# One written order for all five engines through the whole attention stage, with the engine of each copy named in it

## The chip, the cores and the metric

One core of one Trainium2 chip. The metric is the device time of one execution in microseconds (us), the median of the runs shown; lower is better. The engines are TensorE (PE; its weight loads are PEld), VectorE (DVE), ScalarE (ACT), GpSimd (POOL) and SyncE (SP), each of which works through its own instructions in order. DMAs are issued from the queues of SP, ACT and POOL.

## The reference

Three layers follow each other on 2304 = 4 x 576 rows, all in float32. This is `reference()`, cut to what is computed:

```python
# attention: 4 batches, 8 heads, 512 local and 32 global rows, head size 64, window 32
s_g   = scale * q_g @ concat(k_g, k_l).T            # global rows see everything
out_g = softmax(s_g) @ concat(v_g, v_l)
s_ll  = where(|i - j| <= 32, scale * q_l @ k_l.T, -1e9)
out_l = softmax(concat(scale * q_l @ k_g.T, s_ll)) @ concat(v_g, v_l)
x = concat(out_g, out_l) as [2304, 512]
# feed-forward 1, 1536 wide
xn = x / sqrt(mean(x*x) + 1e-6) * rms_g
x  = (silu(xn @ w_gate) * (xn @ w_val)) @ w_out
# feed-forward 2, 2048 wide
h  = x @ w_in
x  = ((a0 + a1*h + a2*h^2 + a3*h^3) / (1 + |b0||h| + |b1|h^2 + 1e-6)) @ w_out
```

The weights arrive as float64 and are turned on the chip into two float32r halves (the "conversion").

## The kernel before

The attention works in 32 stages (`Attention.place`): a stage is one pair of heads and 256 local rows. A stage has four steps on PE: `scores` (S, into a PSUM tile psS), `trans` (T, psT), `pv` (O, psO) and `out` (X, psX). Between them lie masks and sums on DVE, exponentials and copies on ACT. Once per batch `make_g` (psKG) turns the global keys and queries, eight times `g_scores`, `g_trans`, `g_pv` and `g_out` (psG, psGT, psOg, psGX) treat the global rows. Values lie in four buffers `vw`: `load_v` brings a stage's values to partitions 32 to 63, `spread_v` copies them to two other groups of 32 partitions (`vw<-vw`).

Beside it runs the first feed-forward layer (`FFN1`). Its work is cut into units: 12 matmuls of a gate and a value half (`up`, psg and psv), or 12 matmuls of a product with w_out (`down`, psA). 12 units make one of 8 blocks of rows for one of 3 groups of 512 columns. 58 units run inside the attention, so that PE has something dense to do while a stage waits. Before a block's first unit come its norm (`norm_stages`: psN, a small chain of DVE and ACT operations on the tile `sm`, psR, four scalings of x) and its split in two halves (`chunk`, xt).

The order is set in two ways. For the first 14 stages, 18 units, the conversion of the first 12 weights and three norms, a text `SCRIPT` (L857) is read token by token: `S4` is the first step of stage 4 on PE, `M4` its masks on DVE, `E4` its exponentials, `>q5` a load on SP's queue, `U` a unit, `n0` the next step of a norm. All five engines take their instructions in the order of the text. From stage 14 on, the loop at L1038 calls `flow` (L553), which puts loads, steps, units and norm steps one behind the other; PE and SP keep that order, while ACT, DVE and POOL are ordered by a list scheduler when the program is built. Which engine does a copy is fixed in the code: `spread_v` for stages 4 and up is two DMAs on SP's queue, psT and psX are emptied by ACT, psGT and psGX by DVE, the key blocks of the global rows are copied by POOL, and in the conversion `CONV_ON` (L879) names the engine for three of the operations.

```python
        self.advance(t - 1, 2)          # flow: T of the stage before
        between()                       # a unit
        self.advance(t, 1)              # S of this stage
        self.advance(t - 2, 4)          # X
        self.advance(t - 1, 3)          # O
        self.ready(t + 1)               # keys and queries of the next
        between()
        middle()                        # a step of a norm
```

After the attention the rest of the units, the conversion of the other weights and the second feed-forward layer are ordered by the list scheduler.

Of the kernel before, what the change touches and what calls it, by code (L numbers as in the profile page):

```python
# [10 lines left out]
F32 = mybir.dt.float32  # L11
# [9 lines left out]
S = SL + SG  # L21
# [25 lines left out]
class Weights:  # L47
# [30 lines left out]
    def stages(self, job, lo_eng, r8_act, sum_eng=None):  # L78
# [6 lines left out]
        if self.wide:  # L85
# [4 lines left out]
            if r8_act:  # L90
# [6 lines left out]
            nc.vector.tensor_scalar(out=vf, in0=vf, scalar1=TINY, scalar2=None, op0=ALU.max)  # L97
            nc.vector.tensor_scalar(
                out=v, in0=v, scalar1=3, scalar2=0x3FFFFFFF, op0=ALU.logical_shift_left, op1=ALU.bitwise_and
            )  # L100
            nc.vector.scalar_tensor_tensor(
# [3 lines left out]
            (sum_eng or nc.vector).tensor_tensor(out=v, in0=v, in1=lo, op=ALU.add)  # L105
        else:
            yield
            yield 1
            yield 1
# [5 lines left out]
        lo_eng.tensor_tensor(out=out[:, 1], in0=vf, in1=out[:, 0].bitcast(F32), op=ALU.subtract)  # L115
# [29 lines left out]

def pool_round(nc):
    return lambda out, in_: nc.gpsimd.tensor_scalar(  # L147
        out=out, in0=in_, scalar1=1.0, scalar2=1.0, op0=ALU.mult, op1=ALU.mult
    )


class Attention:
# [9 lines left out]
    def __init__(self, tc, pool, x, stage, q_l, k_l, v_l, q_g, k_g, v_g, ident):  # L162
        self.tc, self.nc, self.pool, self.x = tc, tc.nc, pool, x
# [159 lines left out]
    def make_k(self, r):  # L323
# [3 lines left out]
        if r < 4:  # L327
# [3 lines left out]
            nc.vector.tensor_copy(out, ps.rearrange("p (m i k) -> p m i k", i=2, k=32))  # L331
        else:
# [3 lines left out]
        nc.gpsimd.tensor_scalar(  # L336
            out=_ap(kt, [[32 * (KBLK - 8), 2], [32, 8], [1, 32]]), in0=_ap(kg, [[0, 2], [0, 8], [1, 32]]),
            scalar1=1.0, scalar2=1.0, op0=ALU.mult, op1=ALU.mult,
        )

    def make_q(self, s):
        nc = self.nc
        self.qts[s] = qt = self.pool.tile([128, 256], F32, tag="qt", name=f"qt{s}", bufs=2)
        if s < 8:
# [3 lines left out]
            nc.scalar.activation(out=qt, in_=ps[:, 0:256], func=AF.Copy)  # L348
# [55 lines left out]
    def trans(self, s):  # L404
# [5 lines left out]
        nc.scalar.activation(out=o, in_=ps, func=AF.Copy)  # L410

    def pv(self, s):
# [15 lines left out]
        nc.vector.reciprocal(out=dn, in_=dn)  # L428
        self.on[s] = on = self.work.tile([128, 4, D], F32, tag="on", name=f"on{s}", bufs=2)
        nc.vector.tensor_tensor(out=on, in0=ps[:, :, 0:D], in1=_ap(dn, [[1, 4], [0, D]]), op=ALU.mult)  # L430

    def out(self, s):
# [8 lines left out]
        nc.scalar.activation(out=xo, in_=ps[:, 0:256], func=AF.Copy)  # L441
# [25 lines left out]
    def g_trans(self, qd, part):  # L467
# [10 lines left out]
        nc.vector.tensor_copy(o[:, g0:g1], ps[:, 0 : 128 * (g1 - g0)].rearrange("k (n q) -> k n q", q=128))  # L478

    def g_pv(self, qd):  # L480
        nc, o, ps = self.nc, self.gq.pop(qd), self.bank(2, f"psOg{qd}")
        for n in range(5):
# [11 lines left out]
        nc.vector.reciprocal(out=gs[:, 0:1], in_=gs[:, 0:1])  # L494
        og = self.pool.tile([128, 2, D], F32, tag="og", name=f"og{qd}", bufs=1)
        self.gq[qd] = og
        nc.vector.tensor_scalar(
            out=og, in0=_ap(ps, [[0, 2], [1, D]]), scalar1=gs[:, 0:1], scalar2=None, op0=ALU.mult
        )

    def g_out(self, qd):
# [4 lines left out]
        for hf in range(2):  # L506
            rows = slice(64 * hf, 64 * hf + 64)
            src = ps[rows, 0:128].rearrange("d (p h i) -> d p h i", p=2, h=2)[:, :, hf, :]
            self.nc.vector.tensor_copy(self.x[b][hq][rows, :, 0:SG], src)

    def all(self, gen):
        for _ in gen:
            pass

    def advance(self, s, to):

        if not 0 <= s < self.NS:
            return
        while self.stage.get(s, 0) < to:
            now = self.stage[s] = self.stage.get(s, 0) + 1  # L520
            self.all((self.scores, self.trans, self.pv, self.out)[now - 1](s))
            if now == 3 and s + 4 < self.NS:
                self.load_v(s + 4)

    def ready(self, t):

        b, i = divmod(t, 8)
        if t >= self.NS:
            return
        if i < 4 and b:  # L530
            self.all(self.make_k(4 * b + i))
            if i < 2:
                self.load_k(4 * b + i + 2)
        self.all(self.make_q(t))

    def loads(self, t):

        b, i = divmod(t, 8)
        if t >= self.NS:
            return  # L540
        if t + 1 < self.NS:
            self.spread_v(t + 1)
        if b + 1 < B:
            if i == 4:
                self.load_g(b + 1)
            if i in (5, 6):
                self.load_k(4 * b + i - 1)
            if i >= 4:
                self.load_q(8 * b + i + 4)
        if t > 7 and i in (3, 4, 5):  # L550
            self.load_vn(4 * b + i - 3)

    def flow(self, t, between, middle):  # L553

        NS = self.NS
        b, i = divmod(t, 8)
        live = t < NS
        qd = 2 * b
        self.loads(t)
        self.advance(t - 1, 2)  # L560
        between()
        if live and i in (6, 7):
            self.all(self.g_pv(qd + i - 6))
            if i == 6:
                self.load_vn(2 * qd + 3)
        if live and i in (5, 6):
            self.all(self.g_trans(qd + i - 5, 0))
        self.advance(t, 1)
        if live and i in (5, 6):
            self.all(self.g_trans(qd + i - 5, 1))  # L570
        self.advance(t - 2, 4)
        self.advance(t - 1, 3)
        if live and i == 6 and b + 1 < B:
            self.all(self.make_g(b + 1))
        self.ready(t + 1)
        between()
        middle()
        if live and i in (4, 5):
            self.all(self.g_scores(qd + i - 4))
        if i == 0:  # L580
            self.all(self.g_out(qd - 1))
        if live and i == 7:
            self.all(self.g_out(qd))
        between()


class FFN1:
# [6 lines left out]
    def __init__(self, tc, pool, x, y, gam, wts, ident):  # L594
        self.tc, self.lo = tc, tc.nc.gpsimd
# [7 lines left out]
        self.norms, self.acts, self.split_of, self.pending, self.copies, self.defer = {}, {}, {0: {}, 1: {}}, {}, {}, True  # L603
# [21 lines left out]
    def norm_stages(self, blk):  # L625
# [7 lines left out]
        for c, q in ((1, r), (2, u), (3, r)):  # L633
            nc.scalar.activation(out=q, in_=self.xs(blk, c), func=AF.Square)
            yield
            self.lo.tensor_tensor(out=m, in0=m, in1=q, op=ALU.add)
# [40 lines left out]
    def chunk(self, grp, blk, c, xt):  # L677
# [6 lines left out]
        self.lo.tensor_tensor(out=t[:, 1], in0=v, in1=t[:, 0].bitcast(F32), op=ALU.subtract)  # L684
# [14 lines left out]
    def act(self, k, blk, pss, use_silu):  # L699
# [16 lines left out]
        self.lo.tensor_tensor(out=al, in0=a, in1=ah.bitcast(F32), op=ALU.subtract)  # L716

    def down(self, grp, blk, m):
# [12 lines left out]
        if grp == 0:  # L731
            nc.scalar.activation(out=y, in_=ps, func=AF.Copy)
# [123 lines left out]

SCRIPT = """  # L857
>k0 i1 i0 }q0 >g0 }q1 >k1 ]v0 tab i2 K0 >k2 i3 k0 Q0 q0 >q2 H0 h0 Q1 >k3 j0 z0 q1
S0 >w1 >v1 K1 M0 E0 k1 z1 s0 T0 S1 C0 GS0 M1 E1 >q3 Q2 GM0 K2 q2 O0 >w0 k2 z2
K3 GE0 >v2 N0 T1 S2 k3 z3 C1 a1 M2 X0 GS1 E2 s1 T2 Y0 >v3 GM1 l1 GT0 n0 C2 GC0  # L860
Q3 b1 GT1 q3 O1 GE1 S3 >v5 N1 a0 d1 l0 >w2 M3 X1 s2 E3 >w3 GC1 >c b0 T3 Y1 f1
>q4 C3 s3 O2 n0 d0 >n0 f0 N2 >v4 e0 n0 X2 O3 Y2 e1 n0 >q5 N3 Q4 n0 q4 >v6 a2
X3 S4 l2 a3 b2 >n1 Y3 l3 Q5 >s4 n0 q5 M4 n0 S5 E4 >q6 b3 d2 n0 >s6 T4 f2 >s5
n0 M5 GO0 d3 n0 C4 >w5 n0 E5 e2 O4 >q7 GN0 n0 f3 GT2 >q8 N4 GX0 e3 n0 GC2 GY0 X4
>n2 a5 l5 n0 GT3 Y4 n0 >w6 Q7 GC3 b5 >g1 q7 Q6 T5 q6 >w4 S7 C5 >v7 n0 d5 n0 x0
S6 x1 M7 >v8 x2 y0 O5 E7 M6 y1 H1 N5 T7 y2 x3 >v9 f5 U y3 h1 C7 Q8 e5 a4
j1 E6 >w7 U Q12 >s8 l4 b4 >k4 T6 a6 U l6 b6 C6 d4 u0 >s7 O6 f4 u0 U >w8 d6
>g2 N6 u0 e4 f6 K4 >w9 X5 u1 X6 >q9 Y5 O7 u1 e6 Y6 a7 U N7 l7 u0 a8 b7 >n3
# [278 lines left out]
```

## Time and profile before

| | us |
|---|---|
| median of 3 runs | 1016.77 (1015.79 to 1017.24) |
| the profiled execution: its own time | 1017.83 |
| the profiled execution: its span | 1016.0 |
| attention stage with its 58 units, up to | about 270 |
| TensorE clock granted, mean of the span | 0.97 |

The profiled execution lies 1.06 us above the median, and 1.83 us of its time lie outside the span. Shares of busy time are read by stretch, since the attention (0 to 270 us) and the feed-forward layers (270 to 1016 us) have little in common: in the second part PE is busy nearly all the time.

### The profile page before, as it was taken

The page shows a single profiled execution, that of the slowest core. Times are in us where ns is not written, and L with a number is a line of the kernel's source. Part 1 is how long each engine was busy: PE and PEld are TensorE (multiplying, and loading weights), DVE is VectorE, ACT ScalarE, POOL GpSimd, SP SyncE. Part 2 cuts the span into 40 slices and gives each one's busy share as a digit, 9 for nine tenths or more (in the row PEclk, how much of TensorE's full clock was granted, in tenths as well). Part 3 has the DMA queues.
Part 4 walks back from the last instruction along what each step waited for, and adds up shares of the span by engine and source line. Part 5 has one row for each costly group of instructions (what it writes and reads, how often), then busy time and mean ns, then how long its engine had stood idle before and what let it go on. Part 6 is the DMA issues. An engine that isn't in the chain of part 4 may idle for free.

```text
span 1016.0 us, 21488 instructions
## 1 busy us (share of the span) xinstructions
PE 957.9 (94%) x8224; PEld 877.4 (86%) x8224; DVE 778.3 (77%) x1856; ACT 578.9 (57%) x1319; POOL 279.5 (28%) x351
## 2 busy tenths in 40 slices
PE   6778998789999999999999999999999999999997
PEld 4576877677899999899999998888989899898995
DVE  6878555555698997738964535998998989989897
ACT  6566354345676765436632424666666666666674
POOL 6666132121200000000000012453543435434433
PEclk9587999789999999999999999999999999999999
DMA  8887665443535216404310135000000000000000
GB/s 176 209 174 163 131 127 119 103 96 80 181 132 166 85 63 209 166 1 167 125 43 1 43 96 195 1 1 32 1 1 32 1 18 15 1 32 1 1 32 21
DMA packets 132614, 82.24 MB, mean 81 GB/s; under 512 B 95424, under 2 KB 120032, under 8 KB 132512
## 3 DMA queue, kind: packets, MB, share of 16 engines
q1 hardware_dynamic: 129536, 74.02, 26.6%
q0 software_dynamic: 1888, 6.59, 2.0%
q8 instruction: 65, 1.06, 0.4%
q10 hardware_dynamic: 1088, 0.26, 0.1%
q14 instruction: 37, 0.30, 0.1%
HBM read 62.64 MB, written 10.75 MB: 72 GB/s over the span
## 4 chain that ended last, share of the span: by engine, by line
PE 64%; DVE 17%; DMA 7%; SPq 4%; ACT 4%; issue 2%; POOL 1%; ACTq 0%; DVEq 0%; POOLq 0%
PE psA L725 4%; PE psg L693 4%; PE psA L727 4%; PE psA L726 4%; PE psv L693 4%; PE psg L697 4%; PE psg L694 4%; PE psv L694 4%; PE psv L697 4%; SPq L215 4%; PE psH L804 4%; PE psH L805 4%; PE psH L806 4%; PE psB L839 4%; PE psB L840 3%; PE psB L841 3%
## 5 line engine op out<-in xcount | busy, mean ns | idle before, releaser
L804 PE MATMUL psH<-yt,w_h 128*128 128x384 f32 (+1 forms) x384 | 126.0, 329 | 1.2 <-ACT yt L786 0.7
L805 PE MATMUL psH<-yt,w_h 128*128 128x384 f32 (+1 forms) x384 | 125.4, 327 | 0.0
L806 PE MATMUL psH<-yt,w_h 128*128 128x384 f32 (+1 forms) x384 | 123.5, 328 | 0.8 <-DVE yt L787 0.8
L693 PE MATMUL psg<-xt,w_g 128*128 128x288 f32 (+1 forms) x384 | 116.3, 304 | 0.0
L725 PE MATMUL psA<-ah,w_o 128*128 128x288 f32 (+1 forms) x384 | 110.9, 293 | 5.4 <-ACT ah L714 2.8
L147 POOL TENSOR_SCALAR gh<-p 128x384 fp32r<-128x384 f32 (+1 forms) x96 | 57.7, 601 | 211.8 <-DVE p L828 178.4
L693 PE MATMUL psv<-xt,w_v 128*128 128x288 f32 (+1 forms) x384 | 112.2, 293 | 0.3 <-DVE gm L460 0.3
L839 PE MATMUL psB<-w_p,gh 128*128 128x512 f32 x272 | 107.8, 396 | 4.9 <-POOL gh L147 4.8
L694 PE MATMUL psg<-xt,w_g 128*128 128x288 f32 (+1 forms) x384 | 111.9, 292 | 0.0
L694 PE MATMUL psv<-xt,w_v 128*128 128x288 f32 (+1 forms) x384 | 111.9, 292 | 0.0
L726 PE MATMUL psA<-ah,w_o 128*128 128x288 f32 (+1 forms) x384 | 109.1, 288 | 0.0
L727 PE MATMUL psA<-al,w_o 128*128 128x288 f32 (+1 forms) x384 | 109.0, 288 | 0.0
L830 POOL TENSOR_TENSOR gl<-p,gh 128x384 fp32r<-128x384 f32 (+1 forms) x96 | 106.2, 1106 | 8.4 <-PE psB L841 0.5
L840 PE MATMUL psB<-w_p,gh 128*128 128x512 f32 x272 | 107.2, 394 | 0.0
L697 PE MATMUL psg<-xt,w_g 128*128 128x288 f32 (+1 forms) x384 | 106.0, 292 | 0.0
L697 PE MATMUL psv<-xt,w_v 128*128 128x288 f32 (+1 forms) x384 | 105.8, 293 | 0.0
L824 ACT ACTIVATE r<-q,cq 128x384 f32<-128x384 f32 (+1 forms) x96 | 57.4, 598 | 63.8 <-DVE q L814 63.0
L93 POOL TENSOR_SCALAR raw_h<-raw_h 128x512 int32<-128x512 uint32 x1 | 0.6, 647 | 328.4 <-DMA raw_h<-in_moe_w_in_dram 328.4
L814 DVE SCALAR_TENSOR_TENSOR q<-q,bv,t 128x384 f32<-128x384 f32 (+1 forms) x96 | 71.4, 744 | 22.5 <-ACT q L812 22.5
L841 PE MATMUL psB<-w_p,gl 128*128 128x512 f32 x272 | 82.0, 394 | 0.0
L725 PEld LDWEIGHTS psA<-ah,w_o 128*128 128x128 f32 x384 | 71.9, 188 | 7.8 <-ACT ah L714 3.5
L813 ACT ACTIVATE p<-psH,av 128x384 f32<-128x384 f32 (+1 forms) x96 | 62.7, 653 | 26.3 <-POOL gl L830 26.0
(173 smaller groups left out, 2638.5 us busy)
## 6 DMA issues: line engine op xcount, KB each, us to landing
raw_h<-in_moe_w_in_dram SPq DMA_DIRECT2D x16, 512.0 KB, 3.9
raw_p<-in_moe_w_out_dram SPq DMA_DIRECT2D x16, 512.0 KB, 3.9
vw<-vw SPq DMA_DIRECT2D x56, 130.0 KB, 2.4
raw_v<-in_moe_w_val_dram SPq DMA_DIRECT2D x12, 512.0 KB, 5.1
raw_g<-in_moe_w_gate_dram SPq DMA_DIRECT2D x12, 512.0 KB, 6.2
raw_o<-in_moe_w_out_dram SPq DMA_DIRECT2D x12, 512.0 KB, 3.9
vw<-in_v_l_dram SPq DMA_DIRECT2D x60, 80.0 KB, 2.7
out_dram<-o SPq DMA_DIRECT2D x17, 256.0 KB, 2.0
```

Source lines behind the costliest of these rows:

```text
L693: nc.tensor.matmul(ps[j], part(j, 0, c), xt[c][:, 0], start=(c == 0), stop=False)
L694: nc.tensor.matmul(ps[j], part(j, 1, c), xt[c][:, 0], start=False, stop=False)
L697: nc.tensor.matmul(ps[j], part(j, 0, c), xt[c][:, 1], start=False, stop=(c == 3))
L725: nc.tensor.matmul(ps, wh, ah, start=(i == 0), stop=False)
L726: nc.tensor.matmul(ps, wl, ah, start=False, stop=False)
L727: nc.tensor.matmul(ps, wh, al, start=False, stop=(i == 3))
L804: nc.tensor.matmul(ph[:, :n], wh, yt[:, c, 0, :n], start=(c == 0), stop=False)
L805: nc.tensor.matmul(ph[:, :n], wl, yt[:, c, 0, :n], start=False, stop=False)
L806: nc.tensor.matmul(ph[:, :n], wh, yt[:, c, 1, :n], start=False, stop=(c == 3))
L839: nc.tensor.matmul(acc[m], gh[:, sl], wh, start=(k == 0), stop=False)
L840: nc.tensor.matmul(acc[m], gh[:, sl], wl, start=False, stop=False)
L841: nc.tensor.matmul(acc[m], gl[:, sl], wh, start=False, stop=(k == NC2 - 1))
```

## The change

The text `SCRIPT` now covers all 32 stages, all 8 norms and all 58 units, and the five engines follow it to the end of the attention. `flow`, `ready`, `loads`, `advance` and the loop around them are gone. A token may end in `/A`, `/V` or `/P`, which names ACT, DVE or POOL for the operation (`self.eng`); `]` in front of a load names POOL's queue. Helper `put` writes the copy for the engine named. Each step of a conversion is now its own token. In the norm the first estimate r0 and its first refinement lie in PSUM (behind the sums in psN) and no longer in the SBUF tile `sm`.

```diff
+def put(nc, eng, out, in_):
+    if eng == "A":
+        nc.scalar.activation(out=out, in_=in_, func=AF.Copy)
+    elif eng == "V":
+        nc.vector.tensor_copy(out, in_)
+    else:
+        nc.gpsimd.tensor_scalar(out=out, in0=in_, scalar1=1.0, scalar2=1.0, op0=ALU.mult, op1=ALU.mult)
...
-            (sum_eng or nc.vector).tensor_tensor(out=v, in0=v, in1=lo, op=ALU.add)
+            (nc.gpsimd if self.eng == "P" else nc.vector).tensor_tensor(out=v, in0=v, in1=lo, op=ALU.add)
...
     def spread_v(self, s):
-            if s < 4:
-                self.nc.gpsimd.tensor_scalar(out=out, in0=in_, scalar1=1.0, scalar2=1.0, op0=ALU.mult, op1=ALU.mult)
+            if self.eng:
+                put(self.nc, self.eng, out, in_)
             else:
                 self.dma(out=out, in_=in_)
...
-        nc.scalar.activation(out=o, in_=ps, func=AF.Copy)
+        put(nc, self.eng or "A", o, ps)
...
-        nc.vector.tensor_tensor(out=on, in0=ps[:, :, 0:D], in1=_ap(dn, [[1, 4], [0, D]]), op=ALU.mult)
+        if self.eng == "A":
+            for i in range(4):
+                nc.scalar.activation(out=on[:, i], in_=ps[:, i, 0:D], func=AF.Copy, scale=dn[:, i : i + 1])
+        else:
+            nc.vector.tensor_tensor(out=on, in0=ps[:, :, 0:D], in1=_ap(dn, [[1, 4], [0, D]]), op=ALU.mult)
...
-        nc.scalar.activation(out=r, in_=m.bitcast(I32), func=AF.Exp, scale=-self.LN2H / 2**23, bias=self.eps)
+        r0 = ps[:, 4 : 4 + n]
+        nc.scalar.activation(out=r0, in_=m.bitcast(I32), func=AF.Exp, scale=-self.LN2H / 2**23, bias=self.eps)
...
-S6 x1 M7 >v8 x2 y0 O5 E7 M6 y1 H1 N5 T7 y2 x3 >v9 f5 U y3 h1 C7 Q8 e5 a4
+q7/V X5 t2 S7 Y5/A y3/P U M7 >n2 y2/P E7 d2/V >v8 H1 b5 f2 U h1 o5 e2/V T7 t5 u0 U a4 j1 >q6 C7/A d5/V l4/A >k4
...
-    manual.enter_context(tc.manual_schedule(engines={mybir.EngineType.PE, mybir.EngineType.SP}))
...
+        tc.manual_schedule(engines={getattr(mybir.EngineType, e) for e in ("PE", "SP", "Activation", "DVE", "Pool")})
...
-    for t in range(FLOW, LAST + 1):
...
-            att.flow(t, between, norm_step)
...
+    assert done[0] == IN_ATTN
```

PE, the norm of block 4, before: the sums (psN) and the spread of the result over the partitions (psR) stand next to each other, between a unit (psg, psv) and the turning of stage 26's probabilities (psT). The same holds for blocks 2, 5 and 7.

```order
L697 MATMUL psg_3_3478<-xt_2_3_2780,w_g_1058 128x288
L697 MATMUL psv_3_3479<-xt_2_3_2780,w_v_1178 128x288
L641 MATMUL psN_3582<-ones,st_4_3459 128x1 x3
L657 MATMUL psR_3595<-ident,sm_3586 128x128 x2
L657 MATMUL psR_3595<-ident,sm_3586 128x32
L407 MATMUL psT_3607<-ident,p_3516 128x128 x4
```

And after, around the same block's psN, where a transposition of the global rows and their product (psOg) follow:

```order
L495 MATMUL psGT_1_4175<-ident,pg 128x128 x2
L455 MATMUL psX_4182<-ident,on_4170 128x128 x2
L590 MATMUL psN_4187<-ones,st_4_4031 128x1 x3
L526 MATMUL psGX_4194<-ident,og_4151 128x128
L503 MATMUL psOg_4196<-vn_105,ptg_4146 32x64 x2
```

Its psR comes 37 rows later, behind psOg (20 matmuls), a unit of block 5, another psGX and a second unit:

```order
L648 MATMUL psv_2_4222<-xt_5_2_3536,w_v_975 128x256
L648 MATMUL psg_2_4221<-xt_5_3_3577,w_g_1053 128x256
L648 MATMUL psv_2_4222<-xt_5_3_3577,w_v_975 128x256
L608 MATMUL psR_4271<-ident,sm_4217 128x128 x2
L608 MATMUL psR_4271<-ident,sm_4217 128x32
```

For blocks 2, 5 and 7 it comes 60, 63 and 120 rows later; nothing stands next to its own psN any more.

SP's queue, before, around the loads of the queries of batch 3 (x_0_76) and of the keys (kin): spreads (`vw<-vw`) stand in front of both.

```order
L215 DMA vw_100<-vw_100 32x2x520 x2
L215 DMA gin<-in_k_g_dram 32x8x64
L215 DMA gin<-in_q_g_dram 32x8x64
L215 DMA x_0_76<-in_q_l_dram 32x16x32 x4
L215 DMA vn_103<-in_v_l_dram 128x2x256
L215 DMA vn_103<-in_v_g_dram 32x2x64
L215 DMA vw_102<-in_v_l_dram 32x10x64 x2
L215 DMA vw_101<-vw_101 32x2x520 x2
L215 DMA kin_88<-in_k_l_dram 32x16x32 x4
```

After, the same loads on SP's queue:

```order
L232 DMA vw_101<-in_v_g_dram 32x8x64 x2
L232 DMA kin_88<-in_k_l_dram 32x16x32 x4
L232 DMA x_1_75<-in_q_l_dram 32x16x32 x4
L232 DMA vw_100<-in_v_l_dram 32x10x64 x2
L232 DMA x_1_77<-in_q_l_dram 32x16x32 x4
L232 DMA x_0_76<-in_q_l_dram 32x16x32 x4
```

and on POOL, which did no DMAs in this stretch before, loads and spreads between the subtractions of the units:

```order
L667 TENSOR_TENSOR al_3_2214<-a_3_2212,ah_3_2213 128x288
L232 DMA vw_102<-in_v_l_dram 32x10x64 x2
L232 DMA vw_102<-in_v_g_dram 32x8x64 x2
L232 DMA vw_101<-vw_101 32x2x520 x2
L667 TENSOR_TENSOR al_0_2305<-a_0_2303,ah_0_2304 128x256
L159 TENSOR_SCALAR vw_102<-vw_102 32x2x520 x2
L232 DMA kin_88<-in_k_l_dram 32x16x32 x4
L585 TENSOR_TENSOR st_2_2291<-st_2_2291,st_2_2293 128x288
```

Counted over the program, SP issues 114 DMAs fewer: 88 went to POOL's queue (20 of kin, 40 of values and global values to vw, 14 of vn, 14 spreads) and 26 spreads became copies. Of the 64 spread copies and DMAs 30 are DMAs now (56 before), 20 copies on POOL (8) and 14 on ACT (0).

## Rows read from the trace of the kernel before

**Rows 1.** The page: span, TensorE's granted clock in 40 slices of 25.4 us.

```profile
span 1016.0 us, 21488 instructions
PEclk9587999789999999999999999999999999999999
```

**Rows 2.** Busy time by stretch: length, PE, PEld, DVE, ACT, POOL, clock, DMA share, GB/s.

```profile
0.00:122.00 122.00, 96.16 (x1410) 76.10 (x1410) 90.43 (x311) 69.75 (x182) 67.01 (x91) 0.83 0.78 173
122.00:270.00 148.00, 130.05 (x2089) 111.78 (x2086) 78.66 (x354) 70.35 (x204) 37.39 (x52) 0.93 0.46 101
270.00:1016.00 746.00, 731.72 (x4733) 689.53 (x4731) 609.20 (x1191) 438.82 (x934) 175.13 (x209) 1.00 0.18 62
```

**Rows 3.** Waits of PE, 122 to 270 us: waiter, awaited: sum us, times, longest.

```profile
PE psR L657 <- DVE sm L652: 8.6, 4, 2.8
PE psKG L356 <- ACT x L441: 2.1, 1, 2.1
PE psX L436 <- DVE x L509: 1.3, 1, 1.3
```

**Rows 4.** Time line of PE at block 4's norm: start, length, instruction, idle before.

```profile
218.17 0.72 PE L641 MATMUL psN<-ones,st 128*128 128x1 f32 x6
221.70 1.46 PE L657 MATMUL psR<-ident,sm 128*128 128x128 f32 x6 [2.81 <-DVE sm L652]
```

**Rows 5.** The three stretches at half clock after 122 us (columns of rows 2).

```profile
155.65:159.06 3.41, 3.41 (x19) 3.41 (x19) 1.79 (x4) 0.60 (x1) 0.00 (x0) 0.50 0.00 0
186.37:196.61 10.24, 8.39 (x65) 8.06 (x67) 4.07 (x15) 1.30 (x3) 1.66 (x3) 0.50 0.41 85
220.50:227.33 6.83, 5.63 (x54) 5.31 (x54) 2.78 (x7) 0.60 (x1) 0.64 (x1) 0.50 0.10 31
```

**Rows 6.** Time line of PE where the clock falls, at 186.4 us.

```profile
185.98 0.29 PE L694 MATMUL psg<-xt,w_g 128*128 128x288 f32 x1
186.11 0.29 PE L693 MATMUL psv<-xt,w_v 128*128 128x288 f32 x1
...
186.60 0.45 PE L694 MATMUL psg<-xt,w_g 128*128 128x288 f32 x1
186.84 0.45 PE L693 MATMUL psv<-xt,w_v 128*128 128x288 f32 x1
```

**Rows 7.** Chain of waits that ended last, 180 to 186 us: start, length, what.

```profile
180.79 0.49 SPq L215
...
181.32 2.25 DMA kin<-in_k_l_dram
...
185.35 0.46 PE psKG L356 x4
```

**Rows 8.** DMA issues up to 270 us: queue, count, KB each, median us to landing.

```profile
vw<-in_v_l_dram SPq DMA_DIRECT2D x60, 80.0 KB, 2.7
vw<-in_v_l_dram POOLq DMA_DIRECT2D x2, 80.0 KB, 3.7
```

**Rows 9.** Spreads, 0 to 270 us: ns least/median/most of one, first and last start.

```profile
L215 SPq DMA_DIRECT2D vw<-vw x56: 591/596/1640, 32.1 to 238.8; - x56
L304 POOL TENSOR_SCALAR vw<-vw x8: 1048/1054/1398, 8.4 to 26.4; 32x1040 f32<-32x1040 f32 x8
```

**Rows 10.** Groups of POOL, 0 to 270 us: busy us, mean ns, idle before.

```profile
L716 POOL TENSOR_TENSOR al<-a,ah 128x256 fp32r<-128x256 f32 x12 | 9.1, 762 | 15.6 <-PE psA L727 10.9 <-ACT ah L714 4.6
L105 POOL TENSOR_TENSOR cv<-cv,raw_o 128x512 int32<-128x512 int32 x4 | 5.5, 1370 | 2.1 <-POOL al L716 0.7 <-DVE cv L101 0.7 <-issue 0.7
L215 POOL DMA_DIRECT2D vw<-in_v_l_dram x2 | 1.5, 738 | 0.0
```

**Rows 11.** Groups of DVE: up to 122 us (first row), over the whole span (others).

```profile
L105 DVE CUSTOM_DVE_ANT_0 cv<-raw_g,cv 128x1024 uint16<-128x1024 uint16 x1 | 1.3, 1319 | 0.1
...
L684 DVE TENSOR_TENSOR xt<-x,xt 128x256 fp32r<-128x256 f32 x36 | 14.6, 418 | 3.2 <-ACT xt L682 3.2
L105 DVE CUSTOM_DVE_ANT_0 cv<-raw_o,cv 128x1024 uint16<-128x1024 uint16 x8 | 5.5, 684 | 0.0
```

More of the change, by code (lines that the diff above doesn't have):

```diff
@@ L494, in g_pv @@
         nc.vector.reciprocal(out=gs[:, 0:1], in_=gs[:, 0:1])
+        yield
         og = self.pool.tile([128, 2, D], F32, tag="og", name=f"og{qd}", bufs=1)
         self.gq[qd] = og
-        nc.vector.tensor_scalar(
-            out=og, in0=_ap(ps, [[0, 2], [1, D]]), scalar1=gs[:, 0:1], scalar2=None, op0=ALU.mult
-        )
+        two = _ap(ps, [[0, 2], [1, D]])
+        if self.eng == "A":
+            nc.scalar.activation(out=og, in_=two, func=AF.Copy, scale=gs[:, 0:1])
+        else:
+            nc.vector.tensor_scalar(out=og, in0=two, scalar1=gs[:, 0:1], scalar2=None, op0=ALU.mult)
     def g_out(self, qd):
@@ L508, in g_out @@
             src = ps[rows, 0:128].rearrange("d (p h i) -> d p h i", p=2, h=2)[:, :, hf, :]
[L509 to L584, printed above, removed]
+            put(self.nc, self.eng or "V", self.x[b][hq][rows, :, 0:SG], src)
@@ L602, in __init__, with pick @@
         self.ident = ident
-        self.norms, self.acts, self.split_of, self.pending, self.copies, self.defer = {}, {}, {0: {}, 1: {}}, {}, {}, True
+        self.norms, self.acts, self.split_of, self.pending, self.copies, self.defer = {}, {}, {i: {} for i in range(TASKS)}, {}, {}, True
+    def pick(self):
+        return {"V": self.nc.vector, "P": self.nc.gpsimd}.get(self.eng, self.lo)
     def set_psum(self, pp, gv, acc):
@@ L1005 @@
             att.spread_v(n)
-        elif name in ("a", "l", "b", "d", "f", "e"):
+        elif name in "abdefolt":
             if name == "a":
-                pick = [{"A": None, "P": nc.gpsimd, "V": nc.vector}[e] for e in CONV_ON[n]]
-                conv[n] = wts.stages(jobs[n], pick[2], not pick[0], pick[1])
+                conv[n] = wts.stages(jobs[n], nc.gpsimd, True)
             next(conv[n], None)
@@ L1019 @@
             next(phases["x", n], None)
-        elif name in ("U", "D"):
+        elif name == "U":
             unit()
         elif name == "W":
-            next(ffn.copies[1, n], None)
+            next(ffn.copies[divmod(n, 4)], None)
         elif name == "u":
@@ L1030 @@
             next(phases[then[name], n], None)
-    for s in range(FLOW):
-        att.stage[s] = sum((n, s) in phases for n in "STOX")
-    begin.close()
     ffn.defer = False
@@ L1036 @@
         assert next(rest, 0) == 0
-    base = done[0]
-    for t in range(FLOW, LAST + 1):
-        for _ in range(2):
-            wts.step(nc.gpsimd)
-        if t < HALF:
-            target[0] = base + (EARLY - base) * (t + 1 - FLOW) / (HALF - FLOW)
-        else:
-            target[0] = EARLY + (IN_ATTN - EARLY) * (t + 1 - HALF) / (LAST + 1 - HALF)
-        with tc.high_priority(offset=50):
-            att.flow(t, between, norm_step)
-        while done[0] < target[0] - 1:
-            unit()
-        if t % 4 == 1:
-            norms.append(ffn.norm(ORD[(t - 5) // 4]))
-        with tc.high_priority(offset=200):
-            norm_step()
-    while done[0] < IN_ATTN:
-        unit()
+    att.eng = ffn.eng = wts.eng = None
+    assert done[0] == IN_ATTN
     manual.close()
```

127 lines of the change are left out of this document (75 added, 52 removed).

## The prediction

> **What bounds the kernel now.** I read the shares by stretch first [rows 2]. From 270 us on PE is busy for 731.72 of 746 us at full clock; the change touches nothing there and I expect the same time. What can be won lies before: in the first 122 us, which already follow a written order, PE is idle for 122 - 96.2 = 25.8 us and the granted clock is 0.83; from 122 to 270 us, where the list scheduler orders ACT, DVE and POOL, it is idle for 148 - 130.1 = 17.9 us and the clock is 0.93. In that second stretch no other engine is near its limit: DVE is busy for 78.7 of 148 us, ACT for 70.4, POOL for 37.4, and the DMAs have a share of 0.46. So it is not work that holds PE up there, but the order in which short steps wait for each other.
>
> The waits of PE say which [rows 3]: 8.6 us in four waits of psR for the small chain of the norm (`sm`, L652), 2.1 us in one wait of psKG for ACT and 1.3 us in one of psX for DVE; together 12.0 of the 17.9 us. One of them in the time line [rows 4]: psN starts at 218.17 and lasts 0.72 us, psR starts at 221.70, after 2.81 us of idleness. Nothing is late in it; the chain through DVE and ACT takes 2.8 us, and PE's own order has nothing else to do in between. It costs a second time through the clock [rows 1, 5]: after 122 us PE is at the lower level, 1.2 GHz, in three stretches of 20.48 us together, with 17.4 us of busy PE in them, and each begins at such a place. The one from 155.65 follows a wait of psR, the one from 186.37 follows the wait of psKG and holds another psR, the one from 220.50 lies in the wait of rows 4.
>
> **The change, part by part.** The norms first. In the new order of PE the four psR that stood next to their psN stand 37 to 120 rows behind it, with two units or more, or the steps of several stages, between. A unit is 12 matmuls of 256 or 288 columns, and at full clock one starts 0.13 us after the other [rows 6], so two units are 24 x 0.13 = 3.1 us, more than the longest of the four waits. I take 8.0 of the 8.6 us as gone; the bounds are 4 us (DVE and ACT reach the chain late, because they too have other things in their lists) and 8.6. Late next is what needs the scaled x, the split of a block whose units come later, and those have units of the block before them as cover. That the norm's r0 goes to PSUM I cost at nothing: the chain is covered, and without that cover it would cost at most what it costs today.
>
> The clock. Two matmuls are 0.13 us apart at full clock and 0.24 us apart at the lower level [rows 6]. If the three stretches vanish, 17.4 us of busy PE become 17.4 x 0.13 / 0.24 = 9.4 us: 8.0 us at most, and 0 at least, if other gaps pull the clock down in their place. The new order has its own thin places: between units 46 and 47 nine steps of stages follow each other without a unit. One dip of the size of the last (5.6 us of busy PE, 2.6 us of loss) I leave standing: 8.0 - 2.6 = 5.4 us.
>
> The loads. The wait of psKG hangs on a chain that starts in SP's queue [rows 7]: SP issues one DMA after the other at half a microsecond each, the keys' load starts only at 181.32 and takes 2.25 us, the DVE waits for it with all that is behind it, and psKG starts at 185.35. SP loses 114 issues; the 40 spreads among them at 0.596 us [rows 9] and the others at 0.49 us [rows 7] are 23.8 + 36.3 = 60 us of queue time, and the loads of queries and keys no longer stand behind spreads that wait for a stage's pv. I take 3 us of the 2.1 + 1.3 us [rows 3]; bounds 0 and 3.4.
>
> What it adds. POOL issues 88 DMAs at 0.74 us [rows 10], 65 us, and makes 12 spreads more at 1.05 us [rows 9], 12.6 us; it loses 30 subtractions and sums of norms at about 0.76 us and 9 sums of the conversion at 1.37 us [rows 10], 35 us, and 8 key copies, at a spread's 1.05 us at most 8.4 us. Its 104 us of work before 270 us [rows 2] become about 140: room is left. DVE takes on the 30 subtractions at 0.42 us, 12.5 us, and 9 sums at 0.68 to 1.32 us [rows 11], 6 to 12 us, with copies of 4000 columns net that I price by the same 0.42 us for 256 columns, 6.5 us: its 169 us [rows 2] become about 195 to 200. Over 253 us that is 78%, and in the first stretch it goes from 90.4 to about 97 to 102 of 122 us. That is the cost that I trust least; for the first stretch as a whole I take 0, with -10 us (its idle time and its lower clock are both larger than after 122 us, and the loads come earlier) and +10 us (the DVE's work lies wholly on the path) as bounds. ACT's 14 spreads appear in no row on that engine. The nearest is POOL's, 1.05 us, which I take: 15 us, on an engine that is busy for 140 of 270 us [rows 2]; half of it and twice it change nothing.
>
> Sum: 8.0 + 5.4 + 3 + 0 = 16.4 us off the profiled execution's 1017.83 us. It lies 1.06 us above the median, so for the median 1016.8 - 16.4 = 1000.4, rounded to **1000 us**. About 0.2%, 2 us, is what a measurement of this kernel can tell from no change.
>
> **The rivals.** (a) The first stretch gains as well. Its 25.8 us of idle PE and its clock of 0.83 (0.17 x 122 = 21 us of clock not granted) are larger than all that I count after 122 us, and now every engine's place in it is chosen anew. A third of them, about 15 us, on top gives 985. Against it: the DMAs (0.78 of the time) and DVE (90.4 of 122 us) are near their limit there [rows 2], and DVE gets more.
>
> (b) DVE becomes the bound. If the 7 to 12 us that it gains in the first stretch come out on PE, and some waits for copies that ACT made before come on top, of 16.4 us some 4 are left: 1013. For it speaks that one list for DVE holds work of five kinds, each of which can stand in front of the other; against it, that DVE has 148 - 78.7 us free after 122 us.
>
> (c) POOL's queue is late, and the kernel is slower. A stage's values and keys are now often loaded from POOL's queue, where they stand behind subtractions that wait for units, and a load that waits for a buffer holds up the subtractions behind it, on which the next units hang. The two such loads in the trace took 3.7 us to land, against 2.7 from SP [rows 8], and issuing costs 0.74 us of POOL's own time. If each of the 18 stages after the fourteenth waits 1.5 us for this, that is 27 us: 16.4 - 27, thus 1027 us. It decides from 16.4 / 1.5 = 11 late stages on. Against it: SP's spread of a stage took part in the waits, too, and most of POOL's loads stand some stages ahead of their use. The Trainium skill ("SBUF — State Buffer", section "SBUF: two separate sides") has a rule that speaks for it: descriptors of a DMA issued from GpSimd are written by that engine's own cores, which are locked out while VectorE runs an operation that takes both ports, so that the transfer starts late; it advises SP's or ACT's queue. By that rule the time would be that of (c); by the trace, where the two loads land 1.0 us later, loads that are issued some stages ahead hide it and the sum stays. Two loads are few to tell the two apart.
>
> (d) That the change does not do what it says can be left out: the orders above show the moved instructions.
>
> **How the numbers follow.** The forecast has 0.55: its own range, from the bounds of its three terms with a third of the bounds of the first stretch (4 + 2 + 0 to 8.6 + 8 + 3.4 + 3), goes from 994 to 1011. (a) has 0.20, (b) 0.13, (c) 0.12. Faster by over 0.2% are the forecast, (a) and half of (b): 0.82. Within 0.2% lies 0.06 of (b); slower are (c) and no more: 0.12. For 8 in 10 the range takes in (a) down to 982 and (b) up to 1015 and leaves out (c) and the far end of (a).
>
> **What would show it.** Right: PE waits of psR after 122 us under 1 us in all; no wait of psKG behind a load of keys; clock at 0.97 or more from 122 us to the end of unit 58, and that end at about 253 us instead of 270; from there on 746 us as before; DVE near 195 us by then. Wrong: psT, psO or psS waiting for DVE or POOL by more than 8 us in all; DMA landings from POOL's queue in the chain of waits; a clock in the second stretch that is no better than 0.93; or an end of the first stretch that moves by more than 10 us in either direction.

## The result and the profile after

| | before | after |
|---|---|---|
| median of the runs beside each other, us | 1016.28 (4 runs) | 1000.54 (4 runs, 998.86 to 1005.71) |
| ratio, with its 95% interval | | 0.985 [0.981, 0.989] |
| the same comparison on a second chip | 1019.04 (11 runs) | 1001.22 (6 runs), 0.983 [0.979, 0.986] |
| profiled execution: span, us | 1016.0 | 997.4 |

The kernel is faster by 1.5%, and the forecast of 1000 us and its range hold. The page of the changed kernel, where [rows 1] stood before:

```profile
span 997.4 us, 21577 instructions
PEclk9788999999899999999999999999999999999999
```

The clock row has no 5 in it any more, and behind the first four slices a single 8, at about 250 us. The busy time by stretch, with the columns of [rows 2], cut at unit 9 (which starts at 96.1 us before and 96.2 us after) and at unit 72 (289.5 before, 271.2 after). First the kernel before:

```profile
0.00:96.00 96.00, 72.25 (x1145) 54.16 (x1145) 76.71 (x265) 59.66 (x154) 59.35 (x82) 0.80 0.82 185
96.00:289.50 193.50, 173.46 (x2512) 153.21 (x2505) 111.08 (x447) 98.26 (x270) 45.86 (x62) 0.94 0.53 130
```

The changed kernel:

```profile
0.00:96.00 96.00, 68.49 (x1119) 50.87 (x1119) 68.19 (x268) 64.00 (x170) 47.59 (x73) 0.86 0.82 186
96.00:271.20 175.20, 163.62 (x2531) 147.56 (x2531) 133.80 (x498) 121.10 (x327) 87.87 (x125) 0.97 0.49 123
122.00:224.00 102.00, 99.57 (x1776) 87.33 (x1774) 75.43 (x323) 71.71 (x205) 60.95 (x89) 1.00 0.41 90
224.00:254.00 30.00, 22.10 (x212) 21.00 (x213) 24.62 (x67) 21.78 (x52) 5.71 (x7) 0.84 0.75 272
```

By unit 72 both kernels have done the same work on PE, and the changed one is there 18.3 us earlier; from there to the end they take 726.5 and 726.2 us. (Just ahead of unit 72 matmuls of several units stand between each other, so its start can be placed to about 1 us only.) Of the 18.3 us only 4.7 are less idleness of PE (43.8 us before, 39.1 after: length less busy time, over both stretches); 13.6 are less busy time for the same matmuls. From 122 to 224 us PE now has full clock and is idle for 2.4 of 102 us. From 224 to 254 us it is idle for 7.9 of 30 us at a clock of 0.84: here something was lost. The waits of PE from 122 to 254 us, as in [rows 3]:

```profile
PE psR L608 <- DVE sm L603: 5.5, 1, 5.5
PE psA L676 <- DVE x L614: 2.0, 1, 2.0
PE psO L432 <- ACT vw L155: 1.8, 1, 1.8
```

The four waits of psR of [rows 3] are gone, and so is psKG's. One wait of psR is new and longer than any of them: that of block 6, the last norm, at 240.8 us.

Because execution times scatter by several us, I read the experiments by stretches of PE's work as well, from the starts of units in the time lines of their profiled executions. Each run has the kernel before beside it on its own chip, and the ratio is to that:

| kernel | ratio to before, 95% interval | start of unit 19 | 19 to 58 | 58 to 72 | 72 to end |
|---|---|---|---|---|---|
| before | | 119.5 | 146.0 | 24.0 | 726.5 |
| changed | 0.985 [0.981, 0.989] | 123.9 | 114.5 | 32.8 | 726.2 |
| changed, second chip | 0.983 [0.979, 0.986] | 125.2 | 114.4 | 32.2 | 727.0 |
| e1 norm apart (on before) | 0.991 [0.988, 0.993] | 119.1 | 136.6 | 24.1 | 725.0 |
| e2 norm together | 0.997 [0.995, 1.000] | 123.7 | 129.6 | 32.0 | 731.7 |
| e3 loads on SP | 0.989 [0.986, 0.991] | 126.7 | 113.0 | 33.6 | 730.0 |
| e4 no engine names | 0.988 [0.986, 0.991] | 127.0 | 116.3 | 32.8 | 726.4 |
| e5 last norm later | 0.984 [0.980, 0.988] | 124.9 | 113.6 | 31.6 | 730.8 |
| e6 queries earlier | 0.982 [0.979, 0.986] | 122.4 | 114.4 | 32.2 | 726.6 |
| e7 refined earlier | 0.982 [0.980, 0.985] | 124.9 | 112.4 | 32.7 | 727.5 |
| e9 conversion held | 0.981 [0.979, 0.983] | 123.1 | 113.6 | 29.4 | 724.8 |
| e10 held, norm later | 0.976 [0.974, 0.978] | 127.3 | 114.1 | 26.9 | 724.5 |
| e11 held on both | 0.971 [0.967, 0.975] | 125.8 | 113.4 | 25.2 | 725.3 |
| e12 all | 0.971 [0.968, 0.974] | 123.9 | 113.4 | 24.0 | 724.6 |

Two things have to be known for it. The code up to unit 19 is the same in the changed kernel, its repetition, e5, e9, e10 and e11, and unit 19 starts there at 123.1 to 127.3 us: a difference of 2 us in that column says nothing. And at unit 19 the changed kernel has begun 16 stages, the kernel before 14. Two stages are 188 matmuls of the attention; at 0.037 to 0.052 us for each (the 114.5 or 146.0 us, less 39 units of 12 x 0.13 us, over the 1465 or 1647 matmuls that follow) that is an estimate of 7 to 10 us. So of the 31.5 us that the stretch from 19 to 58 lost, 22 to 25 are real, 3 to 5 were gained before unit 19, and 8.8 were given back between units 58 and 72.

### The profile page after: what moved, and what is told of

It is laid out like the page before. It is cut to its first block, busy times and chain, and to the rows that moved or that the text cites. A ratio compares the mean times of both kernels' runs of the same rounds, so it can differ in the third digit from the quotient of the medians.

```text
span 997.4 us, 21577 instructions
## 1 busy us (share of the span) xinstructions
PE 944.8 (95%) x8224; PEld 868.6 (87%) x8224; DVE 784.7 (79%) x1891; ACT 601.8 (60%) x1382; POOL 311.5 (31%) x406
## 4 chain that ended last, share of the span: by engine, by line
PE 65%; DVE 16%; DMA 7%; ACT 4%; SPq 4%; issue 2%; POOL 2%; ACTq 0%; POOLq 0%; DVEq 0%
PE psg L644 4%; PE psA L676 4%; PE psA L678 4%; PE psA L677 4%; PE psv L644 4%; PE psg L648 4%; PE psg L645 4%; PE psv L648 4%; PE psv L645 4%; PE psH L755 4%; PE psH L756 4%; PE psH L757 4%; PE psB L790 4%; PE psB L791 4%; PE psB L792 4%; SPq L232 3%
## 5 line engine op out<-in xcount | busy, mean ns | idle before, releaser
L765 DVE SCALAR_TENSOR_TENSOR q<-q,bv,t 128x384 f32<-128x384 f32 (+1 forms) x96 | 68.5, 713 | 21.9 <-ACT q L763 21.7
L755 PEld LDWEIGHTS psH<-yt,w_h 128*128 128x128 f32 x384 | 72.2, 188 | 5.3 <-DVE p L767 1.5
```

The source lines that it names most:

```text
L755: nc.tensor.matmul(ph[:, :n], wh, yt[:, c, 0, :n], start=(c == 0), stop=False)
```

## The experiments

**The norm's place alone, in the kernel before.** The end of a norm comes one stage behind its psN:

```diff
         if t % 4 == 1:
             norms.append(ffn.norm(ORD[(t - 5) // 4]))
-        with tc.high_priority(offset=200):
-            norm_step()
+            with tc.high_priority(offset=200):
+                norm_step()
```

> Kernel before with one edit: the last steps of a norm (refinement, psR, scalings of x) come one stage later than psN instead of right behind it. Theory (the norm's chain on PE's own order was the main loss after 122 us): the four psR waits, 8.6 us, fall below 1.5 us, the half-clock stretches at 155.6, 186.4 and 220.5 us shrink from 20.5 to under 10 us, and the time falls by 9 to 13 us, to 1003 to 1007. Rival (loads, queues and the choice of engines carry the gain; PE finds the next wait as soon as psR's is gone): psR's waits fall as well, but psT, psS, psKG or psX wait in their place and the time falls by 3 us at most, to 1013 or more.

Measured: 1007.18 us, ratio 0.991; by the ratio that is 9.3 us less than before. The waits of PE from 122 to 270 us:

```profile
PE psA L725 <- DVE og L497: 3.6, 1, 3.6
PE psX L436 <- DMA x<-in_q_l_dram: 2.4, 1, 2.4
PE psX L436 <- DVE x L509: 2.2, 1, 2.2
PE psN L641 <- DVE a L712: 1.6, 1, 1.6
PE psA L725 <- DVE on L430: 1.3, 1, 1.3
PE psR L657 <- ACT y L732: 0.5, 1, 0.5
```

The waits of psR fell from 8.6 to 0.5 us. psA and psX took much of it (9.5 us in the four rows, 3.2 us before), yet 9.4 us remain from unit 19 to 58: 5.6 us of idle time of PE and 3.8 us of busy time of the same 2118 matmuls. After 122 us the half-clock stretches fell from 20.5 to 13.7 us. psKG's wait fell from 2.1 to 0.3 us, though no load moved. One edit of two lines gives over half of what the change gives.

**And the other way round.** In the changed kernel psR goes back next to psN for blocks 2, 5, 4 and 7 (for 2 and 5 psN and the chain move down to psR, for 4 and 7 the rest of the norm moves up to psN). For block 4 (`n5`):

```diff
-GC15/V n5 Y29/V u17 GX6 GO7 n5 GY6/V U u17 n5 GN7 u17/P n5 GR7/A GX7 n5 U
+GC15/V n5 n5 n5 n5 n5 n5 n5 n5 n5 n5 Y29/V u17 GX6 GO7 GY6/V U u17 GN7 u17/P GR7/A GX7 U
```

> Changed kernel with one edit: for blocks 2, 5, 4 and 7 psR stands again right behind psN in the written order. Theory (norm's chain): four waits of psR of 2 to 2.8 us each return, 8 to 11 us, and the clock falls at some of them for 3 to 5 us more: 1009 to 1015 against 1000.5. Rival (the other parts of the order carry the gain): the waits return, but PE catches up since it had slack behind them; 1000 to 1004.

Measured: 1013.76 us, ratio 0.997; 12 to 15 us more than the changed kernel's ratios give. The profiled execution lies 5.0 us above that median, and its stretch behind unit 72 is the longest of the table; the reading rests on the stretch before. The waits:

```profile
PE psR L608 <- DVE sm L603: 7.5, 4, 2.0
```

The stretch from unit 19 to 58, with the columns of [rows 2], in the changed kernel:

```profile
123.90:238.40 114.50, 111.85 (x1937) 99.04 (x1935) 83.83 (x349) 79.36 (x231) 62.20 (x91) 1.00 0.43 101
```

and with psR back next to psN:

```profile
123.70:253.30 129.60, 120.08 (x1937) 106.26 (x1936) 87.32 (x353) 80.30 (x233) 63.64 (x93) 0.93 0.38 91
```

Four waits of 7.5 us together made this stretch 15.1 us longer. Over half of that is no idle time: 6.9 us are idle time of PE (9.5 us, 2.6 in the changed kernel) and 8.2 us busy time of the same number of matmuls, at a clock of 0.93 in place of 1.00. A short wait is paid a second time in the matmuls behind it.

**The queue.** 33 tokens change their mark, as in `]v17` to `>v17`; the places stay.

> Changed kernel with the loads and spreads of POOL's queue put on SP's queue at the same places of the text (all but the first). Theory (SP's queue was late, my third term): waits for keys, queries or vw come back, 3 to 5 us, 1003 to 1006. Rival 1 (the place in the text decides, not the queue): within 2 us of 1000.5. Rival 2 (POOL's queue is the later one): faster by 2 us or more, 998 or less.

Measured: 1005.64 us, ratio 0.989. By the ratio it is 3.6 to 6 us slower, but not where the theory had it: from unit 19 to 58 it takes 113.0 us, where the changed kernel, its repetition, e9, e10 and e11 lie between 113.4 and 114.5. What it loses lies before unit 19 (126.7, at the upper edge of the scatter) and behind unit 72 (730.0), in a place that varies by itself (below). So the queue is not what the middle stretch gained by; whether the first stretch needs it stays open. The landings up to 254 us in the changed kernel, with the columns of [rows 8]:

```profile
vw<-in_v_l_dram SPq DMA_DIRECT2D x33, 80.0 KB, 3.6
vw<-in_v_l_dram POOLq DMA_DIRECT2D x29, 80.0 KB, 3.1
vn<-in_v_l_dram SPq DMA_DIRECT2D x9, 256.0 KB, 3.3
vw<-vw SPq DMA_DIRECT2D x16, 130.0 KB, 2.5
vw<-vw POOLq DMA_DIRECT2D x14, 130.0 KB, 3.2
kin<-in_k_l_dram SPq DMA_DIRECT2D x28, 64.0 KB, 3.6
vn<-in_v_l_dram POOLq DMA_DIRECT2D x7, 256.0 KB, 3.6
kin<-in_k_l_dram POOLq DMA_DIRECT2D x20, 64.0 KB, 2.3
```

The landings are mixed. POOL's loads of values (vw) and of keys land 0.5 and 1.3 us sooner than SP's, its loads of vn and its spreads 0.3 and 0.7 us later. With all of them on SP's queue (e3) the values land after 2.8 us and the keys after 2.6.

**The engines.** All `/A`, `/V` and `/P` are taken off (but for the first four spreads), as in `R24/A` to `R24`; 26 spreads become DMAs again.

> Changed kernel with the engine names taken off the text, so that every copy, sum and subtraction goes to the engine that the code of before used (all spreads from stage 4 on are DMAs of SP again); the order of the text is kept. Theory (the order carries the gain): at most 5 us slower than 1000.5, 1000 to 1006. Rival (moving copies between engines and spreads off the DMA queue carries half of it or more): 1008 or more.

Measured: 1005.37 us, ratio 0.988: 3 to 6 us slower by the ratios, 1.8 us from unit 19 to 58. The order carries the gain, the named engines a small part.

**The hand-off, first attempt.** The hand-off is the place where the attention ends and the feed-forward layers go on alone, between units 58 and 59. The last norm's psN and all behind it leave the text:

```diff
-n7 x22 n6 x23 n6 y22/P U u19 n6 y23/P n7 u19 n7 n7 U u19 u18/V n7 u19/V n7 u20 u20 n7 u20 n7 u20/P n7 n7
+x22 n6 x23 n6 y22/P U u19 n6 y23/P u19 U u19 u18/V u19/V u20 u20 u20 u20/P
...
+    norms.append(norm.pop(7))
...
-        norm_step()
+        if n not in (59, 60):
+            norm_step()
```

> The changed kernel itself, unedited, so that the three edits beside it have it on the same chip. Both theories: the same as before, 0.985 of the kernel before; unit 59 starts some 11 us after unit 58, behind one wait of psR of 5.5 us and one of psA of 2.0 us.

> Changed kernel with one edit: of the last norm (block 6, needed only from unit 80 on) psN and all that follows it leave the written order and are done after it, psN before unit 59 and psR three units later. Theory (what the attention won is given back at its end, where the written order makes PE wait for this norm's chain): the wait of psR of 5.5 us and that of psA of 2.0 us go, the half-clock stretch at 244.7 us goes with them (about 3.5 us), and the time falls by 8 to 11 us against the changed kernel on the same chip. Rival (the hand-off is late for another reason: buffers, weights or PSUM banks that the feed-forward layer waits for): PE waits for something else at the same place and the time falls by 3 us at most.

Measured: 1001.22 us for the repetition and 1002.92 us for the edit. The theory falls. PE waits at the same place, now with psN:

```profile
PE psN L590 <- ACT w_v L118: 5.3, 1, 5.3
```

The row names ACT, but psN starts at 246.14 us, when DVE has just ended the last product of unit 58 (`a`, L663, 245.55 to 245.99). After the attention the kernel takes new PSUM tiles, and the first matmul into them waits until the last unit's are read. That was so before, too: psN waited 1.5 us at that place. What had changed is when DVE gets there. The time line of DVE in the changed kernel:

```profile
238.52 0.99 DVE L100 TENSOR_SCALAR cv<-cv 128x512 int32<-128x512 int32 x1
239.43 1.03 DVE L98 TENSOR_SCALAR cv<-cv 128x512 f32<-128x512 f32 x1
240.38 0.15 DVE L595 TENSOR_SCALAR sm<-psN 128x3 f32<-128x3 f32 x1
...
240.78 0.68 DVE L104 SCALAR_TENSOR_TENSOR cv<-raw_g,cv 128x512 int32<-128x512 int32 x1
241.38 0.41 DVE L100 TENSOR_SCALAR cv<-cv 128x512 int32<-128x512 int32 x1
241.72 0.41 DVE L663 SCALAR_TENSOR_TENSOR a<-a,psv 128x256 f32<-128x256 f32 x1
242.05 0.15 DVE L601 SCALAR_TENSOR_TENSOR sm<-psN,sm 128x3 f32<-128x3 f32 x1
242.12 0.67 DVE L108 CUSTOM_DVE_ANT_0 cv<-raw_g,cv 128x1024 uint16<-128x1024 uint16 x1
242.72 0.68 DVE L104 SCALAR_TENSOR_TENSOR cv<-raw_v,cv 128x512 int32<-128x512 int32 x1
243.32 0.14 DVE L602 TENSOR_TENSOR sm<-sm,psN 128x3 f32<-128x3 f32 x1
```

Between two steps of the norm, 0.15 us each, stand steps of the conversion (`cv`) of the next twelve weights, which nobody needs before unit 96. The written order fixes only what it lists; the list scheduler puts the later work in between. And this work can start at all because its loads come earlier now. The first of them on SP's queue, before:

```profile
265.91 0.39 SPq L71 DMA_DIRECT2D raw_g<-in_moe_w_gate_dram  x1
```

and after:

```profile
230.68 0.38 SPq L72 DMA_DIRECT2D raw_g<-in_moe_w_gate_dram  x1
```

These buffers come free with the last step of the attention on PE. Before, it ended at 265.77 us, behind the start of unit 58 (265.5), and DVE's first conversion step came at 270.57 us, after the hand-off. Now it ends at 230.60 us, 7.8 us ahead of unit 58.

**The conversion held back.** In the changed kernel, DVE's steps of what follows are queued behind the last product of unit 58:

```diff
+        self.last_mul = nc.vector.scalar_tensor_tensor(out=a, in0=a, ..., in1=v, op0=ALU.mult, op1=ALU.mult)
...
+    held = ExitStack()
+    held.enter_context(tc.issue_after(ffn.last_mul.ins))
...
         if n == 12 * NB:
+            held.close()
```

> Changed kernel with one edit: the DVE steps of the next weights' conversion, which the list scheduler puts between the steps of the last norm and of the last units, stand behind the last DVE step of unit 58. Nothing else moves. Theory (at the hand-off DVE is the bound: 0.4 to 1.0 us of conversion stand ahead of each short step that PE waits for): the wait of psR falls from 5.5 us to 1.5 to 3 us, unit 59 starts 7 to 9 us after unit 58 instead of 11.3, and 3 to 6 us remain at unit 72. Rival (the conversion is itself needed soon, or the steps wait for ACT): the wait stays above 4.5 us, or PE stops for weights before unit 108; under 1 us.

and the same together with the last norm later:

> The edit of the run before (conversion held back on DVE) together with the last norm taken out of the written order. Theory (PE waits at the hand-off for the last PSUM banks of the attention's pool, which DVE empties behind conversion steps; without these DVE empties them 2 us after unit 58 ends): the wait of psN falls from 5.3 us to 2 us or less, unit 59 starts 5 to 7 us after unit 58, and 5 to 8 us remain at unit 72. Rival (ACT or the loads of weights hold the hand-off): the wait stays above 4 us.

Measured: 995.96 us (ratio 0.981) and 991.07 us (0.976); units 58 to 72 take 29.4 and 26.9 us, against 32.8. In the first, psR's wait is nearly gone, but PE then waits for the scalings of x that the norm ends with:

```profile
PE psA L676 <- DVE x L614: 4.2, 1, 4.2
PE psR L608 <- DVE sm L603: 0.7, 1, 0.7
```

In the second both are out of the way and psN's wait is down to 2.6 us, not to the 2 that I had expected. What is left shows on ACT, in the second kernel:

```profile
242.38 0.69 ACT L92 ACTIVATE raw_g<-raw_g 128x512 int32<-128x512 uint32 x1 [0.42 <-DMA raw_g<-in_moe_w_gate_dram]
243.74 0.65 ACT L92 ACTIVATE raw_v<-raw_v 128x512 int32<-128x512 uint32 x1 [0.67 <-DMA raw_v<-in_moe_w_val_dram]
244.29 0.40 ACT L665 ACTIVATE ah<-a 128x256 fp32r<-128x256 f32 x1
244.60 0.39 ACT L660 ACTIVATE a<-psg 128x288 f32<-128x288 f32 x1
```

The last unit's tanh (L660) stands behind a conversion step that waits for its load of weights. So ACT's steps were held as well (`held.enter_context(tc.issue_after(ffn.last_ah.ins))`, with `last_ah` the copy to `ah`):

> The kernel of the run before (conversion held on DVE, last norm later) with the conversion's ACT steps held behind ACT's last step of unit 58 as well. Theory (an ACT step of the conversion that waits for its load of weights stands ahead of the last units' activations): the wait of psN of 2.6 us falls to 1.5 us or less, unit 59 starts 4 to 4.5 us after unit 58 instead of 5.5, 1 to 2 us at unit 72. Rival (ACT's waits are covered, DVE's chain of the last unit alone sets it): within 0.5 us at unit 72.

Measured: 988.56 us, ratio 0.971, 12 to 15 us less than the changed kernel's ratios give; 7.6 us of it lie between units 58 and 72, and the rest I cannot place (the interval of the ratio is 4 us to either side). psN waits 1.6 us, unit 59 starts 4.0 us after unit 58, as before the change, and units 58 to 72 take 25.2 us (24.0 before):

```profile
PE psN L590 <- DVE a L663: 1.6, 1, 1.6
```

**Two waits of the first stretch.** On SP's queue `>q7` goes ahead of `>s6`:

```diff
-l2/A >s6 X4 b2 n0 GN0 f1 o2 Y4/A >q7 e1/P
+l2/A >q7 >s6 X4 b2 n0 GN0 f1 o2 Y4/A e1/P
```

> Changed kernel with one edit: the load of stage 7's queries stands ahead of stage 6's spread on SP's queue instead of 8 tokens behind it. Theory (SP's queue still delays loads in the first stretch; the spread waits for its buffer and holds up the load): the wait of psQ of 4.6 us at 45.5 us shrinks below 1.5 us and unit 1 starts 3 to 4 us earlier; of that 2 to 5 us remain at the end. Rival (DMA bandwidth and DVE set the pace of the first stretch): the wait goes but the next one grows, and unit 9 starts within 1 us of 96.2; under 1 us at the end.

and on DVE the two refinements of block 0's norm go ahead of a transposition that waits for its load:

```diff
-l11/P Q11 >s10 n1 n2 f9 b11 >s11 n2/P n1 GE2
+l11/P n1 n1 Q11 >s10 n2 f9 b11 >s11 n2/P GE2
```

> Changed kernel with one edit: the two refinements of block 0's norm on DVE stand ahead of stage 11's transposition of queries (which waits for its load) instead of behind it and a conversion step. Theory (the place of short steps in DVE's list sets the wait): the wait of psR at 89.1 us falls from 4.6 to about 2 us, unit 9 starts 2 to 3 us earlier and 1.5 to 4 us remain at the end, the clock included. Rival (what follows, GT and S of stage 12, waits for the same DVE work, so the wait moves there): under 1 us.

Measured: 1000.06 and 1001.00 us, ratio 0.982 both, against 0.983 of the unedited kernel beside them: no difference. psR's wait at 89 us shrank as expected, from 4.6 to 2.1 us. psQ's fell from 4.6 to 1.8 us, but in the repetition of the unedited kernel, too, no wait of psQ is longer than 2.8 us, so that most of this fall lies within the scatter. Unit 9 starts at 96.2 and 97.4 us (96.2 and 96.4 without the edits). Other waits stand there in the second: psOg's of 2.6 us for a conversion step on DVE, and psQ's for loads are 5.8 us (4.6 and 5.0 unedited). Both theories fall. The result is the one that the rivals forecast, that another wait takes the place of the one removed; what sets the pace of the first stretch is not shown.

**All together.**

> All edits that moved a wait together: conversion held on DVE and ACT, last norm later, stage 7's queries earlier, block 0's refinements earlier. Theory (the gains stand at different places of PE's order and add up): 1 to 4 us less than the run beside it at unit 19, and that much at the end, 986 to 990 us. Rival (the first stretch is paced by its DMAs, so that a wait taken away there comes back at the next load): the same as the run beside it within 1 us.

Measured: 987.90 us (987.63 to 989.70), ratio 0.971 [0.968, 0.974], that of the run beside it. The two edits of the first stretch add nothing that can be told; those of the hand-off stay. It is 2.9% faster than the kernel before and beats both kernels.

## Why the prediction was right, step by step

**The total was right through two errors that cancelled.** Forecast: 16.4 us, all gained by the end of unit 58, which was to come at about 253 instead of 270 us. In fact unit 58 starts at 238.4 instead of 265.5 us, 27.1 us earlier; unit 59 at 249.6 instead of 269.5 us, 19.9 us earlier; unit 72 18.3 us earlier. So some 10 us more than forecast were won, and 8.8 us given back, 7.2 of them between units 58 and 59. The text had neither, and that the two come out nearly equal is luck. Of its signs, psKG's (no wait) and the clock's (0.98 from 122 us to unit 59) came true; psR's waits after 122 us, to be under 1 us, are 5.5 us, all at the last norm. DVE was busy for 182 us by then, not 195 to 200, and POOL for 135, not 140.

**The norms (8.0 us) and the clock (5.4 us).** This mechanism was right. The four waits are gone. Done alone they bring 9.4 us (e1), undone they cost 15.1 us (e2); 13.4 lies between. The division was less good: idle and busy time are 5.6 and 3.8 us of the one and 6.9 and 8.2 us of the other. In the change as a whole PE's idle time up to unit 72 fell by no more than 4.7 us, since the hand-off alone has 6.2 us more of it than before, and its busy time fell by 13.6 us. The half-clock stretches up to there fell from 61.4 to 37.5 us; for each kind of matmul the number that ran in them, times what the mean time to the next matmul is longer there, is about 20 us before and 13 to 14 us after, so that 6 to 7 us of the 13.6 are the clock by this estimate. The rest I did not take further. The PSUM place of r0, costed at nothing, did cost nothing on DVE: its steps take 0.14 to 0.16 us there and took 0.15 us before. The low end of the forecast's range counts 2 us for the clock, where its own text had 0 as the bound.

**The loads (3 us).** This step fails. With the loads back on SP's queue the middle stretch is not longer (e3); psKG's wait, on which most of the 3 us hung, is 0.5 us there, and 0.3 us in e1, where no load moved. So it needed neither POOL's queue nor a new place for the loads to go.

**The first stretch (0, from -10 to +10 us).** 3 to 5 us gained, by the estimate above. The written order went two stages further by unit 19; rival (a), at 15 us, was too large.

**From 270 us on, the same.** From unit 72 on, yes: 726.5 and 726.2 us. But the sentence "the change touches nothing there" was the step that failed: the change ends the attention on PE 35.2 us earlier, ahead of the last five units instead of inside the last one, so that the next weights arrive and are converted while the last norm and the last units still need DVE and ACT. Rival (b), DVE as the bound, was expected in the first stretch; it came true here, in the 16 us of DVE's time line from 235 to 251 us.

**Rival (c).** The kernel is not slower, and no late stages show. By the landings alone POOL's queue is neither late nor early, as said above. The Trainium skill ("SBUF — State Buffer", section "SBUF: two separate sides") has the rule that a transfer issued from GpSimd starts late while VectorE runs an operation that takes both ports, and advises SP's or ACT's queue. These landings neither show it nor refute it, since they do not tell at which of them VectorE held the ports; following the advice made no difference from unit 19 to 58 that stands out of the scatter (e3).

Of the gain from unit 19 to 58, 22 to 25 us, the norms are 9 to 15 us and the engines 2; what is left, some 5 to 14 us, lies in the order of the other steps by this subtraction, and no run here takes it apart.

## What to carry to other kernels

A wait of PE of 2 us is worth more than 2 us, when the clock falls behind it (7.5 us of waits cost 15.1 us in e2): count the busy time of the same matmuls before and after, not only the idle time. When a stage ends earlier, look for what its freed buffers set off: loads and conversions that nobody needs yet take their place in front of short steps that everybody waits for, and holding them behind the stage's last short steps, with the last norm moved out of the way, won back 7.6 of 8.8 us. And a written order binds only what it lists; where a scheduler adds the rest, state what must not come in between.

## What the hardware showed that was not expected

Two DVE conversion steps in the time line above took 0.99 and 1.03 us; the same operations on the same tiles took 0.41 (L100, 241.38 us) and 0.42 us (L98, 235.42 us). Beside the slow ones POOL ran two subtractions of two SBUF operands:

```profile
238.42 1.76 POOL L635 TENSOR_TENSOR xt<-x,xt 128x288 fp32r<-128x288 f32 x2 [0.66 <-ACT xt L633]
```

Each of the two DVE steps ended 0.28 us after one of POOL's two, which took 0.88 us each. The same happens elsewhere in this trace, first the DVE step:

```profile
87.26 1.26 DVE L98 TENSOR_SCALAR cv<-cv 128x512 f32<-128x512 f32 x1
```

and the POOL instruction that had started before it:

```profile
86.98 1.26 POOL L121 TENSOR_TENSOR w_o<-cv,w_o 128x512 fp32r<-128x512 f32 x1
```

The trace of the changed kernel has 136 DVE steps of this form. The 125 with no POOL instruction beside them took 0.38 to 0.43 us. Five began 0.10 to 0.48 us after a POOL instruction with its operands in SBUF; they took 0.76 to 1.27 us, and all five ended 0.28 us after that instruction. The other six, beside a POOL instruction that issued a DMA, was about to end, or began with them or later, took 0.38 to 0.47 us. One of the five POOL instructions was a copy with a single operand. The Trainium skill ("SBUF — State Buffer", section "SBUF: two separate sides") states that the two engines share a pair of ports which one of them holds for a whole instruction while the other waits; these rows agree, with DVE as the one that waits. It means that a subtraction moved to POOL to spare DVE may cost DVE as much: here 0.6 us each, where DVE's own subtraction of that form takes 0.46 us (L635, 236.58 us).

In units 120 to 168, where all these kernels do the same, profiled executions took from about 74 us (e10, e11) to about 80 us (e2); in the long ones psA waited up to 2.8 us for ACT. It can account for some us between the medians of kernels with equal attention; its cause was not looked for.
